# Second products of twelve chunks with the output weights held still, in a fused attention and feed-forward kernel

## The chip, the cores and the metric

The kernel runs on one core of one Trainium2 chip. The metric is the device time of one execution in microseconds (us). Before the change it is 499.11 us, the median of three runs (498.87 to 499.72).

## What is computed

First a gated linear attention is run over 768 steps, for 4 batches of 8 heads of size 48. Its output, 3072 tokens of 384 numbers, goes through a feed-forward layer with 2048 hidden units.

```python
for t in range(S):                                   # attention, per batch and head
    state = alpha[:, :, t, :, None] * state + einsum('bhd,bhe->bhde', k[:, :, t], v[:, :, t])
    y[:, :, t] = einsum('bhd,bhde->bhe', q[:, :, t], state)
x = y.transpose(0, 2, 1, 3).reshape(3072, 384)
h = x @ w_in                                         # 384 -> 2048
sp = where(h > 20, h, log1p(exp(min(h, 20))))
out = (h * tanh(sp)) @ w_out                         # 2048 -> 384
```

## The kernel before

**Chunks and units.** The tokens are cut into 24 chunks of 128 columns (64 steps of two batches). A chunk goes through `attention` (VectorE scans of the decay, small matmuls, a state that is carried on), which leaves its 128 columns of `x` in SBUF as a high and a low part (fp32r). The feed-forward layer works in *units*: one block `f` of 128 hidden features (16 of them, `NFF`) for a group of 2 or 4 chunks. There are 100 units. `SEGMENTS` (line 42) lists which groups go over which blocks: chunks 0 to 7 in six pieces (units 0 to 35), since weights and chunks come in one after the other, then chunks 8 to 11, 12 to 15, 16 to 19 and 20 to 23 with all 16 blocks each (units 36 to 51, 52 to 67, 68 to 83, 84 to 99).

**One unit** (`unit`, line 1004). The *first product* (`up`, line 1013) is 9 matmuls: three pieces of the 384 inputs, each as high x high, high x low and low x high. The weights stand still and 512 columns (256 for a group of two) stream. Five ScalarE and VectorE passes make the gate (lines 1026 to 1046), then ScalarE writes the high part of `g` (line 1051) and VectorE the low part (line 1054). The *second product* (`down`, line 1085) is done chunk by chunk: the chunk's 128x128 piece of `g` stands still and the 384 columns of the output weights `wo` stream, three passes per chunk, so 12 matmuls in a unit of four chunks. The sums stay in four PSUM banks (`o0` to `o3`, one for each chunk) over a segment. After the last block ScalarE copies a bank to SBUF with a check sum (`result`, line 1125) and SyncE stores it (line 1131); chunks 0 to 7, whose blocks are spread over segments, are put aside in between (`stash`, `more`, `join`).

**Weights.** They come as 64-bit words (768 KB for a block). VectorE puts the top bits together (lines 428, 433 and 438), ScalarE rounds the high part (line 449), and the low part is the rest. `W_LOW` (line 82) says for each block who computes the low part: `PE` subtracts by two matmuls into a PSUM bank, done once for the input weights and once for the output weights (lines 467 and 468), `POOL` by two GpSimd instructions (line 477), `DVE` by one VectorE instruction (line 455). All weights are loaded once more for a check in the background (line 485).

**Variants of a chunk.** Chunks in `DIRECT` write `x` in place by more matmuls with separate pieces (lines 742 and 781); the others send 16-row pieces through small DMAs (`move`, line 855). In `X_PE` TensorE and ScalarE make the low part of `x` (`off`, line 840) and not VectorE. In `STATE_PE` TensorE adds the state (line 807).

**Order.** `Plan.order` (line 149) goes through all tasks with durations (`COST`) and due times (`key`, with the shifts `DUE_SHIFT`, `W_SHIFT`, `LEAD` and others) and writes down one fixed order for each engine; where its count leaves TensorE idle in the first part it puts in *fills*, matmuls without use (line 1160). The engines then run their orders and wait for each other by semaphores. A unit's second product is due `LAG` = 3 units after its first.

Of the kernel before, what the change touches and what calls it, by code (L numbers as in the profile page):

```python
# [30 lines left out]
P = 128  # L31
# [22 lines left out]
LEAD = 5.5  # L54
SPREAD = 3.0
W_LEAD = 4.25
GATE = -2.0
Q_LEAD = 4.75
V_LEAD = 9.75
FIRST_W = -22.25  # L60
CHECK_FROM = 105
# [5 lines left out]
DUE_SHIFT = {  # L67
# [3 lines left out]
}  # L71
W_SHIFT = {
    0: -30.0, 1: -2.75, 2: -3.75, 3: -1.75, 4: -3.5, 5: -9.25, 6: 0.25, 7: -4.75, 8: 2.5, 9: 2.75,
    10: 2.25, 11: 7.0, 12: -6.25, 13: -7.75, 14: 30.25, 15: -1.75,
}
X_PE = {0, 1}
SIDES = 2
STATE_PE = {2, 6}
PAIR_FROM = 8
BACK_AFTER = 0.8  # L80
# [6 lines left out]
MOVER = {  # L87
    (1, 1, 0): 'ACT', (1, 2, 0): 'ACT', (1, 2, 64): 'ACT', (2, 1, 0): 'ACT', (2, 2, 64): 'ACT',
    (3, 0, 64): 'ACT', (3, 1, 64): 'ACT', (3, 2, 64): 'ACT', (4, 0, 0): 'ACT', (5, 1, 0): 'ACT',
    (6, 0, 0): 'ACT', (6, 0, 64): 'ACT', (6, 2, 64): 'ACT', (8, 0, 0): 'ACT', (8, 1, 64): 'ACT',  # L90
}
# [30 lines left out]
class Plan:  # L122
# [151 lines left out]

KEYS = 60.0
PER_KEY = {'PE': 0.03, 'DVE': 0.02, 'ACT': 0.02, 'POOL': 0.02, 'SP': 0}

# [10 lines left out]
    "front": (1.19, 1.32), "front d": (1.59, 1.72), "front0": (0.76, 0.9), "turn": (0.34, 0.6), "turn2": (0.7, 0.95),  # L288
    "front2": (2.09, 2.22), "back2": (1.91, 2.04), "back2 last": (1.18, 1.3), "spread": (0.4, 0.4),
# [3 lines left out]
    "down": (0.529, 0.8), "stash": (0.4, 0.53), "join": (0.47, 0.59), "result": (0.5, 0.7),  # L293
}
# [15 lines left out]
def fast_path(ctx, tc, qka, v, w, out, good):  # L310
# [48 lines left out]
    gchk = const.tile([P, NFF], F32, name="gchk")  # L359
    n_last = n_chunks - SEGMENTS[-1][1]  # L360
    ws = const.tile([P, 2, NFF, 2, DM], F32R, name="ws")
    wi = ws[:, :, :, 0].rearrange("p z f (s c) -> p z f s c", s=NK)
# [235 lines left out]
    def chunk(n):  # L598
# [54 lines left out]
        if n == 0:  # L653
            got_a, got_k, got_q = (
                add("SP", *COST["load"], -99 + 0.1 * i, load_part(*e), uses=[q_buf], size=230)
                for i, e in enumerate(((a_at, QKA), (k_at, a_at), (0, k_at)))
            )
        elif n < PARTED:
            got_a, got_k = (
                add("SP", *COST["load"], key - Q_LEAD - early, load_part(*e), uses=[q_buf], size=z)  # L660
                for z, e, early in ((230, (a_at, QKA), 1.0), (460, (0, a_at), 0.0))
            )
            got_q = got_k
        else:
            got_a = got_k = got_q = add(
                "SP", *COST["load"], key - Q_LEAD, load, uses=[q_buf], size=692
            )
# [149 lines left out]
        x = xs[tile_at]  # L817
        by_half = lambda t: t.rearrange("p s (t u) -> p u s t", u=2)
        sides = (
# [182 lines left out]
    by_token = out.rearrange("(b t) d -> t b d", t=S)  # L1002

    def unit(c0, nt, f, at, ends):
        N, key = nt * C, float(at)
# [69 lines left out]
        t_lo = add("DVE", *cost("dve"), k + 0.07, lower, [t_hi], [y, g], port=at >= IN_BANK)  # L1075

        for j in range(nt):
            n = c0 + j
# [24 lines left out]
            if f < NFF - 1 and n in kept:  # L1103
                def more(o=o, n=n):
                    nc.vector.tensor_tensor(part[n].tile, o.tile, part[n].tile, ALU.add)

                kept[n] = add("DVE", *COST["join"], k, more, [t_down, kept[n]], [o, part[n]])
                continue
            if f < NFF - 1:
                part[n] = plan.buffer("osb")  # L1110

                def stash(o=o, n=n):
                    nc.scalar.copy(new(part[n], [P, DM], f"part{n}"), o.tile)

# [3 lines left out]
            if from_part:  # L1118
                def join(o=o, n=n):
                    nc.vector.tensor_tensor(part[n].tile, o.tile, part[n].tile, ALU.add)  # L1120

                done = [add("DVE", *COST["join"], k, join, [t_down, kept[n]], [o, part[n]])]
            osb = part[n] if from_part else plan.buffer("osb")

            def result(o=o, n=n, osb=osb, from_part=from_part):
                to = osb.tile if from_part else new(osb, [P, DM], f"osb{n}")
                nc.scalar.activation(
# [3 lines left out]
            def store(n=n, osb=osb):  # L1131
                b, c = chunks[n]
                nc.sync.dma_start(by_token[c * L : (c + 1) * L, 2 * b : 2 * b + 2], osb.tile)

# [8 lines left out]
            def copy(on_act=on_act, o=o, n=n, osb=osb):  # L1143
                to = new(osb, [P, DM], f"osb{n}")
                if on_act:
# [4 lines left out]
            def send(n=n, osb=osb):  # L1150
                b, c = chunks[n]
                queue = nc.scalar if n == n_chunks - 1 else nc.sync
                queue.dma_start(by_token[c * L : (c + 1) * L, 2 * b : 2 * b + 2], osb.tile)

# [245 lines left out]
def lay_out(inputs):  # L1400
# [62 lines left out]
```

## Time and profile before

| | us |
|---|---|
| median of three runs | 499.11 |
| the profiled execution, its own time | 497.71 |
| its span in the profile | 496.0 |
| TensorE busy | 484.6 (98%) |
| ScalarE busy | 382.1 (77%) |
| VectorE busy | 323.1 (65%) |
| GpSimd busy | 25.3 (5%) |

The span runs from the first to the last instruction of the core; 1.71 us of the profiled execution's time lie around it. Busy time of TensorE is that of matmuls whose ends are modelled, and they overlap; how long one really takes of the engine is read from the starts of those that follow each other. "Granted clock" is the share of 2.4 GHz that TensorE got; over the span its mean is 0.998.

### The profile page before, as it was taken

To read this page: it belongs to the slowest core of one execution; us is meant where nothing else is said; L and a number is where in the kernel's file an instruction comes from. 1 tells how busy PE (TensorE), PEld (TensorE's weight loads), DVE (VectorE), ACT (ScalarE), POOL (GpSimd) and SP (SyncE) were. 2 spreads that over 40 slices of the span, in tenths; PEclk is the share of its full clock that TensorE was granted. 3 is DMA by queue.
4 is the path that set the end of the run, shared out by engine and by line. 5 is a ranking of instruction groups with operands and counts; after the bars stand their busy time and mean duration, and the time that the engine had idled before them with its cause. 6 is when DMAs were issued, how large, how long until landed. Compare 5 with 4: busy or idle time off the path is not lost.

```text
span 496.0 us, 12822 instructions
## 1 busy us (share of the span) xinstructions
PE 484.6 (98%) x5319; PEld 432.5 (87%) x5319; DVE 323.1 (65%) x522; ACT 382.1 (77%) x864; POOL 25.3 (5%) x27
## 2 busy tenths in 40 slices
PE   6999999999999999999999999999999999999995
PEld 4688889899899989999989899999989899999994
DVE  7999999999973694447867783863474343343333
ACT  3578786886788778857777897889789899997772
POOL 2003201413000000000000000000000000000000
PEclk9999999999999999999999999999999999999999
DMA  7877544606000250115152543603153412100001
GB/s 248 316 285 236 181 151 157 238 35 214 13 0 9 78 172 1 66 59 175 28 213 75 183 164 99 207 24 118 71 171 93 172 41 106 64 1 0 1 0 68
DMA packets 18926, 56.22 MB, mean 113 GB/s; under 512 B 3440, under 2 KB 11312, under 8 KB 18864
## 3 DMA queue, kind: packets, MB, share of 16 engines
q1 hardware_dynamic: 18592, 55.11, 32.5%
q8 instruction: 42, 0.69, 0.6%
q10 hardware_dynamic: 272, 0.26, 0.2%
q14 instruction: 20, 0.16, 0.1%
HBM read 48.87 MB, written 4.72 MB: 108 GB/s over the span
## 4 chain that ended last, share of the span: by engine, by line
PE 85%; DVE 9%; DMA 3%; issue 1%; ACT 1%; SPq 0%; DVEq 0%; ACTq 0%
PE sums_at L1089 39%; PE h_at L1017 37%; PE att_at L790 2%; PE att_at L752 2%; DVE w_lead L433 2%; PE h_at L763 2%; DMA ws<-in_wp_dram 1%; DVE w_lead L438 1%; PE att_at L724 1%; DMA qka<-in_qka_dram 1%; PE h_at L802 1%; DVE w_lead L428 1%; DVE t L1044 1%; DVE g L1054 1%; DVE rest L672 1%
## 5 line engine op out<-in xcount | busy, mean ns | idle before, releaser
L1089 PE MATMUL sums_at<-ws,g 128*128 128x384 f32 x1152 | 223.9, 340 | 0.1
L1017 PE MATMUL h_at<-xs,ws 128*128 128x512 f32 (+1 forms) x900 | 214.2, 384 | 0.2 <-DVE t L1044 0.2
L1089 PEld LDWEIGHTS sums_at<-ws,g 128*128 128x128 f32 x1152 | 202.4, 188 | 8.1 <-ACT ws L471 0.4
L1017 PEld LDWEIGHTS h_at<-xs,ws 128*128 128x128 f32 x900 | 163.3, 188 | 28.4 <-DVE t L1044 0.5
L1054 DVE SCALAR_TENSOR_TENSOR g<-t,g 128x512 fp32r<-128x512 f32 (+1 forms) x100 | 67.8, 679 | 124.2 <-ACT g L1051 123.9
L1026 ACT ACTIVATE t<-h_at 128x512 f32<-128x512 f32 (+1 forms) x100 | 58.0, 580 | 63.6 <-PE h_at L1017 60.8
L1051 ACT ACTIVATE g<-t 128x512 fp32r<-128x512 f32 (+1 forms) x100 | 60.3, 604 | 11.5 <-PE sums_at L1089 5.3
L1029 ACT ACTIVATE t<-t 128x512 f32<-128x512 f32 (+1 forms) x100 | 61.3, 613 | 2.3
L1032 ACT ACTIVATE t<-t 128x512 f32<-128x512 f32 (+1 forms) x100 | 61.2, 612 | 2.2
L1044 DVE SCALAR_TENSOR_TENSOR t<-t,h_at 128x512 f32<-128x512 f32 (+1 forms) x87 | 57.1, 657 | 8.3 <-ACT t L1035 8.2
L1035 ACT ACTIVATE t<-t 128x512 f32<-128x512 f32 (+1 forms) x100 | 60.4, 604 | 0.5
L672 DVE TENSOR_TENSOR_SCAN rest<-qka,behind 112x520 f32<-112x520 f32 x24 | 30.4, 1268 | 0.4 <-DMA qka<-in_qka_dram 0.2
L685 DVE TENSOR_TENSOR_SCAN qka<-qka,ahead 112x520 f32<-112x520 f32 x24 | 30.6, 1274 | 0.0
L477 POOL TENSOR_TENSOR ws<-w_lead,ws 128x384 fp32r<-128x384 f32 x14 | 22.1, 1598 | 98.3 <-ACT ws L449 98.3
L1026 ACT ACTIVATION_READ_ACCUMULATOR t<-h_at 128x1 f32 x100 | 19.4, 194 | 0.0
L1041 DVE COPY held<-h_at 128x512 f32<-128x512 f32 x13 | 9.0, 691 | 15.8 <-ACT t L1026 15.8
L831 ACT ACTIVATE xs<-att_at 112x384 fp32r<-112x384 f32 (+1 forms) x24 | 12.2, 513 | 6.2 <-PE att_at L809 3.4
L695 DVE TENSOR_TENSOR qka<-qka 112x512 f32<-112x512 f32 x24 | 16.4, 684 | 0.1
L681 DVE TENSOR_TENSOR qka<-qka,rest 112x512 f32<-112x512 f32 x24 | 15.8, 659 | 0.0
L433 DVE SCALAR_TENSOR_TENSOR w_lead<-ws,w_lead 128x768 int32<-128x768 int32 x16 | 15.7, 982 | 0.1
L438 DVE SCALAR_TENSOR_TENSOR w_lead<-ws,w_lead 128x768 int32<-128x768 int32 x16 | 15.3, 957 | 0.1
L449 ACT ACTIVATE ws<-w_lead 128x768 fp32r<-128x768 f32 x16 | 13.4, 839 | 2.3 <-DVE w_lead L438 2.2
(100 smaller groups left out, 366.7 us busy)
## 6 DMA issues: line engine op xcount, KB each, us to landing
qka<-in_qka_dram SPq DMA_DIRECT2D x22, 772.5 KB, 5.8
ws<-in_wp_dram SPq DMA_DIRECT2D x16, 768.0 KB, 4.5
wc<-in_wp_dram SPq DMA_DIRECT2D x16, 768.0 KB, 4.5
v<-in_vp_dram SPq DMA_DIRECT2D x24, 192.0 KB, 4.5
out_dram<-osb SPq DMA_DIRECT2D x15, 192.0 KB, 2.6
xs<-x SPq DMA_DIRECT2D x104, 16.0 KB, 1.8
out_dram<-part SPq DMA_DIRECT2D x8, 192.0 KB, 2.6
qka<-in_qka_dram SPq DMA_DIRECT2D x2, 260.5 KB, 4.4
```

The costliest lines, as they stand in the source:

```text
L433: nc.vector.scalar_tensor_tensor(lead.tile, words(1), -0x40000000, lead.tile, ALU.bitwise_and, ALU.bitwise_or)
L672: nc.vector.tensor_tensor_scan(t[:, :0:-1], alpha()[:, :0:-1], behind[:, ::-1], 0.0, ALU.mult, ALU.max)
L685: nc.vector.tensor_tensor_scan(a, a, ahead, 0.0, ALU.mult, ALU.max)
L1017: nc.tensor.matmul(p[:, :N].rearrange("p (c t) -> p c t", c=nt), wi[:, z, f, s], x[:, :, s, a], start=m == 0, stop=m == len(passes) - 1,)
L1026: nc.scalar.activation(wide(t), wide(h), AF.Exp, accum_out=vchk[:, at : at + 1])
L1029: nc.scalar.activation(wide(t), wide(t), AF.Square, bias=1.0)
L1032: nc.scalar.activation(wide(t), wide(t), AF.Ln, bias=0.2, scale=0.2)
L1035: nc.scalar.activation(wide(t), wide(t), AF.Exp, scale=-1.0)
L1044: nc.vector.scalar_tensor_tensor(wide(y), wide(t), 2.5, wide(held), ALU.subtract, ALU.mult)
L1051: nc.scalar.activation(g.tile[:, 0, :N], wide(y), AF.Copy, scale=-0.4, accum_out=own)
L1054: nc.vector.scalar_tensor_tensor(g.tile[:, 1, :N], wide(y), -0.4, g.tile[:, 0, :N].bitcast(F32), ALU.mult, ALU.subtract,)
L1089: nc.tensor.matmul(o.tile, g.tile[:, a, j * C : (j + 1) * C], wo[:, z, f], start=begins and m == 0, stop=end and m == 2,)
```

## The change

For chunks 8 to 19 (`WIDE`, the groups that begin at 8, 12 and 16) the second product is turned round: 128 output columns of `wo` stand still, the 512 tokens of the group stream, and the result has outputs in its partitions and tokens in its columns. Three banks of 512 columns are used and not four of 384. After the last block VectorE transposes each bank in squares of 32 (`flip`) into a tile of the group, ScalarE makes the check sums over two chunks at a time, and 16 stores of 48 KB take the place of four of 192 KB. So that a square of 32 lands where it can be stored, the host lays the output weights out in another order of columns; the second products that are not turned then read `wo` in 12 runs of 32 columns, and for the three groups the columns of `x` are ordered half by half. SBUF tiles for results hold four chunks (two such tiles in place of eight single ones).

The planner's numbers and choices are set anew as well: due times, costs of loads, and who does what for the early chunks and weights.

```diff
 BUFS = {
-    "h": 2, "t": 3, "g": 2, "osb": 8,
+    "h": 2, "t": 3, "g": 2, "osb": 2,
...
-X_PE = {0, 1}
+X_PE = {0, 1, 2, 4}
-STATE_PE = {2, 6}
+STATE_PE = {2, 3, 4, 6}
-DIRECT = {0, 1, 2, 3, 6, 7}
+DIRECT = {1, 2, 3, 6}
 W_LOW = {
-    0: ('PE', 'o0'), 1: ('PE', 'o0'), 2: ('PE', 'o3'), 3: ('PE', 'o3'), 4: ('POOL', ''), 5: ('PE', 'o0'),
-    6: ('DVE', ''), 7: ('POOL', ''), 8: ('POOL', ''), 9: ('DVE', ''), 10: ('DVE', ''), 11: ('POOL', ''),
-    12: ('POOL', ''), 13: ('POOL', ''), 14: ('DVE', ''), 15: ('POOL', ''),
+    0: ('PE', 'h'), 1: ('PE', 'o3'), 2: ('PE', 'o0'), 3: ('POOL', ''), 4: ('POOL', ''), 5: ('PE', 'o3'),
+    6: ('POOL', ''), 7: ('POOL', ''), 8: ('DVE', ''), 9: ('POOL', ''), 10: ('POOL', ''),
+    11: ('POOL', ''), 12: ('DVE', ''), 13: ('POOL', ''), 14: ('POOL', ''), 15: ('DVE', ''),
 }
+WIDE = {8, 12, 16}
-FLIGHT = 1800.0
+FLIGHT = 3000.0
-DMA_RATE, DMA_FIRST, DMA_LAST = 285.0, 1.1, 0.9
+DMA_RATE, DMA_FIRST, DMA_LAST = 345.0, 1.7, 0.6
...
+        within = "u t" if n // NT_MOST * NT_MOST in WIDE else "t u"
+        by_half = lambda t: t.rearrange(f"p s ({within}) -> p u s t", u=2)
...
+    def wide_products(c0, f, key, g, t_lo):
+        begins, end = f == 0, f == NFF - 1
+        if begins:
+            sums[c0] = [plan.buffer(f"o{i}") for i in range(NK)]
+        turned = out_buffer(c0) if end else None
+        blocks = lambda: out_rows(c0, 4).rearrange("p k (q i e) -> p (k q) i e", i=NK, e=32)
+        flips = []
+        for i, o in enumerate(sums[c0]):
+            def down(o=o, i=i):
+                if begins:
+                    o.tile = sums_at[i]
+                for m, (a, z) in enumerate(((0, 0), (0, 1), (1, 0))):
+                    nc.tensor.matmul(
+                        o.tile, wo[:, z, f, i * P : (i + 1) * P], g.tile[:, a],
+                        start=begins and m == 0, stop=end and m == 2,
+                    )
+            def flip(o=o, i=i):
+                nc.vector.transpose(blocks()[:, :, i], o.tile.rearrange("p (b t) -> p b t", t=32))
...
+        for c in range(2):
+            def check(c=c):
+                rows = out_rows(c0 + 2 * c, 2)
+                nc.scalar.activation(rows, rows, AF.Copy, accum_out=ochk[:, c0 + c : c0 + c + 1])
...
+            for a in range(4):
+                for h in range(2):
+                    def store(a=a, c=c, h=h):
+                        of = blocks()[32 * a : 32 * (a + 1), 8 * c + h : 8 * (c + 1) : 2]
+                        nc.sync.dma_start(
+                            by_block[:, a, c0 // 2 + c, :, h], of.rearrange("p b i e -> p b (i e)")
+                        )
...
+        if c0 in WIDE:
+            wide_products(c0, f, key, g, t_lo)
+            return
...
                     nc.tensor.matmul(
-                        o.tile, g.tile[:, a, j * C : (j + 1) * C], wo[:, z, f],
+                        o.tile.rearrange("p (r i e) -> p r i e", r=4, i=NK),
+                        g.tile[:, a, j * C : (j + 1) * C],
+                        wo[:, z, f].rearrange("p (i r e) -> p r i e", r=4, i=NK),
...
-    wp[:, :, 1] = w_out.reshape(NFF, P, DM)
+    wp[:, :, 1] = (
+        w_out.reshape(NFF, P, 4, NK, 32).transpose(0, 1, 3, 2, 4).reshape(NFF, P, DM)
+    )
```

Three places show what this moves.

TensorE in the group of chunks 12 to 15, second products of units 55 and 56 (`g55`, `g56` are the units' gates, `sums_at` the PSUM banks, `h_at` the bank of a first product). Before:

```order
L1089 MATMUL sums_at0_106<-ws_103,g55_3759 128x384 x3
L1017 MATMUL h_at0_111<-xs1_105,ws_103 128x512 x9
L1089 MATMUL sums_at1_107<-ws_103,g55_3759 128x384 x3
L1089 MATMUL sums_at2_108<-ws_103,g55_3759 128x384 x3
L1089 MATMUL sums_at3_109<-ws_103,g55_3759 128x384 x3
L1089 MATMUL sums_at0_106<-ws_103,g56_3804 128x384 x3
L1017 MATMUL h_at1_112<-xs1_105,ws_103 128x512 x9
```

With the change:

```order
L1036 MATMUL sums_at0_107<-g55_3692,ws_104 128x512 x3
L1086 MATMUL h_at0_112<-xs1_106,ws_104 128x512 x9
L1036 MATMUL sums_at1_108<-g55_3692,ws_104 128x512 x3
L1036 MATMUL sums_at2_109<-g55_3692,ws_104 128x512 x3
L1036 MATMUL sums_at0_107<-g56_3737,ws_104 128x512 x3
L1086 MATMUL h_at1_113<-xs1_106,ws_104 128x512 x9
```

A unit of these groups has three second products of 512 columns and not four of 384. Over the whole program 576 matmuls of 384 columns become 432 of 512, and 576 stay.

GpSimd, low parts of weights (`w_lead4` is block 4). Before:

```order
L477 TENSOR_TENSOR ws_103<-w_lead4_659,ws_103 128x384 x2
L477 TENSOR_TENSOR ws_103<-w_lead7_698,ws_103 128x384 x2
L477 TENSOR_TENSOR ws_103<-w_lead8_1083,ws_103 128x384 x2
L477 TENSOR_TENSOR ws_103<-w_lead13_1339,ws_103 128x384 x2
L477 TENSOR_TENSOR ws_103<-w_lead12_1438,ws_103 128x384 x2
L477 TENSOR_TENSOR ws_103<-w_lead15_1600,ws_103 128x384 x2
L477 TENSOR_TENSOR ws_103<-w_lead11_1623,ws_103 128x384 x2
```

With the change:

```order
L479 TENSOR_TENSOR ws_104<-w_lead3_516,ws_104 128x384 x2
L479 TENSOR_TENSOR ws_104<-w_lead4_608,ws_104 128x384 x2
L479 TENSOR_TENSOR ws_104<-w_lead6_702,ws_104 128x384 x2
L479 TENSOR_TENSOR ws_104<-w_lead7_868,ws_104 128x384 x2
L479 TENSOR_TENSOR ws_104<-w_lead9_1178,ws_104 128x384 x2
L479 TENSOR_TENSOR ws_104<-w_lead10_1251,ws_104 128x384 x2
L479 TENSOR_TENSOR ws_104<-w_lead11_1362,ws_104 128x384 x2
L479 TENSOR_TENSOR ws_104<-w_lead13_1526,ws_104 128x384 x2
L479 TENSOR_TENSOR ws_104<-w_lead14_1773,ws_104 128x384 x2
```

Blocks 3, 6, 9 and 10 come to GpSimd, from TensorE and VectorE; block 8 goes to VectorE. Before, five blocks stood here ahead of the last two, now seven.

VectorE where the group of chunks 8 to 11 ends, with the change (`osb2` is the tile of that group's results, `STREAM_TRANSPOSE` the flip, `t` and `g` the gates of units 52 and 53; `copy_predicated` serves the attention of chunks 18 and 19):

```order
L1110 COPY held53_3415<-h_at1_113 128x512
L1042 STREAM_TRANSPOSE osb2_3488<-sums_at0_107 128x16x32
L1123 SCALAR_TENSOR_TENSOR g52_3421<-t52_3391,g52_3421 128x512
L1113 SCALAR_TENSOR_TENSOR t53_3409<-t53_3409,held53_3415 128x512
L585 COPY_PREDICATED probs_90<-causal_79,h_at0_112 128x2x256
L585 COPY_PREDICATED probs_90<-causal_79,h_at1_113 128x2x256
L1042 STREAM_TRANSPOSE osb2_3488<-sums_at1_108 128x16x32
L1042 STREAM_TRANSPOSE osb2_3488<-sums_at2_109 128x16x32
```

The three flips stand among the gates of the next group's first units; before, nothing of the results of these chunks was on VectorE.

Counted over the program, TensorE also has two subtractions of weights fewer (8 pairs of lines 467 and 468 in place of 10), two additions of a state more, eight small matmuls of line 844 more (12 in place of 4), and 32 fills in place of 31.

## Rows read from the trace of the kernel before

**Rows 1.** The page: busy time of each engine over the span.
```profile
PE 484.6 (98%) x5319; PEld 432.5 (87%) x5319; DVE 323.1 (65%) x522; ACT 382.1 (77%) x864; POOL 25.3 (5%) x27
```
**Rows 2.** Stretches: length, then busy (instructions) of PE, PEld, DVE, ACT, POOL, clock, DMA.
```profile
45.00:95.00 50.00, 49.99 (x793) 44.34 (x793) 49.15 (x77) 39.10 (x94) 13.82 (x8) 1.00 0.55 195
...
400.00:489.00 89.00, 89.00 (x454) 81.22 (x452) 30.95 (x60) 72.46 (x165) 0.00 (x0) 1.00 0.09 30
```
**Rows 3.** The waits of PE, the longest and the last of five: us, times, longest.
```profile
PE sums_at L1165 <- ACT minus_ident L336: 2.8, 1, 2.8
...
PE h_at L1017 <- DVE t L1044: 0.2, 1, 0.2
```
**Rows 4.** The chain that ended last, from 400 us: start, us, what.
```profile
400.76 2.05 PE h_at L1017 x9
402.81 2.10 PE sums_at L1089 x12
404.91 2.08 PE h_at L1017 x9
406.99 2.12 PE sums_at L1089 x12
```
**Rows 5.** PE in order of time from 26 us: start, us, what.
```profile
26.09 0.91 PE L467 MATMUL sums_at<-w_lead,ident 128*128 128x384 f32 x2
...
27.01 0.81 PE L467 MATMUL sums_at<-w_lead,ident 128*128 128x384 f32 x2
...
27.83 0.84 PE L467 MATMUL sums_at<-w_lead,ident 128*128 128x384 f32 x2
...
29.97 0.91 PE L809 MATMUL att_at<-state,ident 112*112 112x192 f32 x4
30.58 0.66 PE L1017 MATMUL h_at<-xs,ws 128*128 128x256 f32 x3
```
**Rows 6.** PE again: line 844, then `back` of a direct chunk, then of another.
```profile
14.35 0.51 PE L844 MATMUL att_at<-xs,minus_ident 128*128 128x192 f32 x2
14.68 0.57 PE L724 MATMUL sums_at<-ident,qka 112*128 112x112 f32 x4
...
28.77 0.58 PE L783 MATMUL att_at<-probs,v_apart 64*64 64x64 f32 x24
...
29.50 0.54 PE L802 MATMUL att_at<-v,ks 64*48 64x48 f32 x32
...
49.14 0.69 PE L790 MATMUL att_at<-probs,v 64*64 64x64 f32 x32
49.63 0.56 PE L802 MATMUL att_at<-v,ks 64*48 64x48 f32 x32
```
**Rows 7.** Groups of PE by line and shape: the fills (busy us, mean ns, idle before).
```profile
L1165 PE MATMUL sums_at<-minus_ident 128*128 128x512 f32 x31 | 10.5, 466 | 2.8 <-ACT minus_ident L336 2.8
```
**Rows 8.** DVE from 71.57 us, and POOL beside it: start, us, what.
```profile
71.57 1.23 DVE L672 TENSOR_TENSOR_SCAN rest<-qka,behind 112x520 f32<-112x520 f32 x1
...
75.67 2.06 DVE L685 TENSOR_TENSOR_SCAN qka<-qka,ahead 112x520 f32<-112x520 f32 x1
...
73.91 2.71 POOL L477 TENSOR_TENSOR ws<-w_lead,ws 128x384 fp32r<-128x384 f32 x2 [21.48 <-ACT ws L449]
```
**Rows 9.** Groups of DVE and ACT by line and shape (busy us, mean ns, idle before).
```profile
L1041 DVE COPY held<-h_at 128x512 f32<-128x512 f32 x13 | 9.0, 691 | 15.8 <-ACT t L1026 15.8
...
L455 DVE TENSOR_TENSOR ws<-w_lead,ws 128x768 fp32r<-128x768 f32 x4 | 3.8, 954 | 0.0
...
L874 DVE TENSOR_TENSOR state<-att_at,state 112x384 f32<-112x384 f32 x4 | 2.2, 552 | 0.0
...
L837 DVE TENSOR_TENSOR xs<-att_at,xs 128x384 fp32r<-128x384 f32 x4 | 2.2, 549 | 0.0
...
L500 ACT ACTIVATE wc<-wc 128x768 f32<-128x768 f32 x16 | 14.6, 915 | 0.0
```
**Rows 10.** Stores of line 1133 on SyncE's queue: min/median/max ns, first and last start.
```profile
L1133 SPq DMA_DIRECT2D out_dram<-osb x12: 539/601/909, 276.1 to 432.2; - x12
```

More of the change, by code (lines that the diff above doesn't have):

```diff
@@ L292 @@
     "x3 hi": (0.16, 0.3), "x3 lo": (0.2, 0.32), "x hi": (0.39, 0.53), "x lo": (0.48, 0.59),
-    "down": (0.529, 0.8), "stash": (0.4, 0.53), "join": (0.47, 0.59), "result": (0.5, 0.7),
+    "down": (0.529, 0.8), "down wide": (0.687, 0.95), "flip": (0.66, 0.8), "sum": (0.87, 1.0), "stash": (0.4, 0.53), "join": (0.47, 0.59), "result": (0.5, 0.7),
 }
@@ L660, in chunk @@
                 add("SP", *COST["load"], key - Q_LEAD - early, load_part(*e), uses=[q_buf], size=z)
-                for z, e, early in ((230, (a_at, QKA), 1.0), (460, (0, a_at), 0.0))
+                for z, e, early in ((267, (a_at, QKA), 1.0), (524, (0, a_at), 0.0))
             )
@@ L1002, in fast_path, with out_buffer, out_rows @@
     by_token = out.rearrange("(b t) d -> t b d", t=S)
+    out_buffers = {}
+    def out_buffer(n):
+        group = n // NT_MOST
+        if group not in out_buffers:
+            out_buffers[group] = plan.buffer("osb")
+        return out_buffers[group]
+    def out_rows(n, count=None):
+        of, place = out_buffer(n), n % NT_MOST
+        if of.tile is None:
+            new(of, [P, NT_MOST, DM], f"osb{n // NT_MOST}")
+        return of.tile[:, place : place + count] if count else of.tile[:, place]
@@ new lines, in fast_path @@
+    by_block = out.rearrange("(b c h t) (a e) -> t a c b h e", b=B, c=NCH, h=2, a=4)
+    def wide_products(c0, f, key, g, t_lo):
[16 more added lines that the diff above has]
+                nc.vector.transpose(blocks()[:, :, i], o.tile.rearrange("p (b t) -> p b t", t=32))
+            t_down = add(
+                "PE", *COST["down wide"], key + LAG + 0.001 * i, down, [t_lo, *ready_w[f, 1]],
+                [g, o], behind=downs.get((c0, i), []), steps=6,
+            )
+            downs[c0, i] = [t_down]
+            if end:
+                flips.append(
+                    add("DVE", *COST["flip"], key + LAG + 0.1 + 0.01 * i, flip, [t_down], [o, turned])
+                )
+        if not end:
+            return
[3 more added lines that the diff above has]
+                nc.scalar.activation(rows, rows, AF.Copy, accum_out=ochk[:, c0 + c : c0 + c + 1])
+            t = add("ACT", *COST["sum"], key + LAG + 0.2 + 0.1 * c, check, flips, [turned])
+            checked.append(t)
+            for a in range(4):
[4 more added lines that the diff above has]
+                            by_block[:, a, c0 // 2 + c, :, h], of.rearrange("p b i e -> p b (i e)")
+                        )
+                    add("SP", *COST["store"], key + LAG + 0.3 + 0.1 * c, store, [t], [turned])
@@ L1104, in more @@
                 def more(o=o, n=n):
-                    nc.vector.tensor_tensor(part[n].tile, o.tile, part[n].tile, ALU.add)
+                    nc.vector.tensor_tensor(out_rows(n), o.tile, out_rows(n), ALU.add)
                 kept[n] = add("DVE", *COST["join"], k, more, [t_down, kept[n]], [o, part[n]])
@@ L1109, in unit @@
             if f < NFF - 1:
-                part[n] = plan.buffer("osb")
+                part[n] = out_buffer(n)
                 def stash(o=o, n=n):
-                    nc.scalar.copy(new(part[n], [P, DM], f"part{n}"), o.tile)
+                    nc.scalar.copy(out_rows(n), o.tile)
                 kept[n] = add("ACT", *COST["stash"], k, stash, [t_down], [o, part[n]])
@@ L1119, in join @@
                 def join(o=o, n=n):
-                    nc.vector.tensor_tensor(part[n].tile, o.tile, part[n].tile, ALU.add)
+                    nc.vector.tensor_tensor(out_rows(n), o.tile, out_rows(n), ALU.add)
                 done = [add("DVE", *COST["join"], k, join, [t_down, kept[n]], [o, part[n]])]
-            osb = part[n] if from_part else plan.buffer("osb")
+            osb = out_buffer(n)
             def result(o=o, n=n, osb=osb, from_part=from_part):
-                to = osb.tile if from_part else new(osb, [P, DM], f"osb{n}")
+                to = out_rows(n)
                 nc.scalar.activation(
@@ L1143, in copy @@
             def copy(on_act=on_act, o=o, n=n, osb=osb):
-                to = new(osb, [P, DM], f"osb{n}")
+                to = out_rows(n)
                 if on_act:
```

40 lines of the change are left out of this document (21 added, 19 removed), and 6 rows, old and new, of the table DUE_SHIFT.

## The prediction

> **What bounds the kernel now.** I read the busy line of the page first: TensorE is busy for 484.6 of the span's 496.0 us, no other engine for more than 382.1 [rows 1]. Then the stretches, because a share over the span says nothing of a stage: from 45 to 95 us TensorE and VectorE are both full (49.99 and 49.15 of 50), from 400 to 489 TensorE is full, VectorE is at 30.95 of 89 and ScalarE at 72.46 [rows 2]. Then TensorE's waits: five lines that add up to 5.5 us, the longest 2.8 on the first constant, all early [rows 3]. Last the chain of waits, where the reader is to see that it is TensorE alone, a first product of 2.05 to 2.08 us and a second one of 2.10 to 2.12 in turn, each starting where the other ends [rows 4]. So the time is the length of TensorE's work, plus 11.4 us (496.0 - 484.6) in which it has none, plus 1.7 outside the span. Work taken from TensorE counts in full as long as nobody makes it wait. In the first 100 us VectorE has only 0.85 us in 50 to spare; there an edit is worth what it takes from both.
>
> **The change part by part.** The sum is made against the profiled execution, 497.71 us; the median of the three runs is 1.40 higher, and I add that at the end.
>
> *(a) Turned products.* A unit of chunks 8 to 19 now has 9 matmuls of 512 columns and not 12 of 384. The nearest row is the first product of the same kernel: also 128x128 held, 512 streaming, 9 in a run. It takes 2.065 us (mean of 2.05 and 2.08), the 12 take 2.11 [rows 4]: 229 and 176 ns for one. Both stream 4608 columns, so the difference is what a matmul costs beside its columns, about 16 ns, paid three times less. 0.045 us in each of 48 units: **-2.16 us**. The bounds are 0 (only the columns count) and -2.9 (2.12 against 2.06). I take the middle, since the form is that of the first product exactly.
>
> The Trainium skill, "TensorE: Matmul & The Clock Gate", section "Wait — 56ns, not 53.3ns?", speaks against this: it has matmuls start every N/2.4 GHz plus about 2.5 ns, so that 9 of 512 would take an estimated 1.94 us and 12 of 384 1.95, and the 48 units would give 0.4 us. The trace disagrees with it in both rows (2.065 and 2.11); the measurement decides, and the rule is a rival below.
>
> *(b to f) TensorE's other work, in the first 100 us.* Two pairs of weight subtractions go: the starts 26.09, 27.01 and 27.83 make one 0.82 to 0.92 [rows 5], so 2 x 0.87 = -1.74. Two chunks more (3 and 4) add their state on TensorE: 29.97 to 30.58 is 0.61 each [rows 5], +1.22. Line 844, 0.33 for a pair of matmuls [rows 6], comes for chunks 2 and 4; a chunk that is not direct (4, and now 0) has a second part a third as wide, 0.11: 2 x 0.33 + 2 x 0.11 = +0.88. Chunks 0 and 7 are no longer direct: a direct `back` takes 0.73 (28.77 to 29.50), another 0.49 [rows 6]; chunk 0 changes once and chunk 7 twice, counting its front, for which I take the same 0.24: -0.72. One fill more: 10.5/31 = +0.34 [rows 7]. Together -0.02: nothing.
>
> *VectorE in the first stretch.* Two state additions (0.55 each), two low parts of `x` (0.55) and two low parts of weights (0.95) fewer [rows 9]: -4.1 us. Against that GpSimd has seven early blocks and not five. Beside GpSimd a scan took 2.06 us and not 1.23 [rows 8], and one block lies on GpSimd for 2.71; with one scan beside each, 2 x 0.83 = +1.7, with two +3.3. Net -2.4 to -0.8: room for VectorE, but by the order it comes late. Ahead of the gates of units 7 to 12 VectorE now has two to six instructions more than before, and fewer only from unit 16 on. I cost this at nothing for TensorE: the lead of a few instructions is given back by unit 16, and TensorE has work of other chunks between those gates. Where that cover is gone, it is the first rival.
>
> *Flips.* Nine new instructions on VectorE. None is in the trace; the nearest are the copy of 512 columns out of PSUM, 691 ns [rows 9], and the scan of 520, 1.23 us [rows 8]. Below: nothing less than the copy, since as many numbers leave the same memory. I take 0.69, 6.2 us in all, and hold 1.23 for the range (11.1 us). What is queued behind them are the gates of the next group's first units, and behind those TensorE's second products, which have three units of slack. The cover is that stage's idle time of VectorE (35% busy without attention [rows 2]; 65% over the span [rows 1]), and that TensorE comes back to a bank only after a first product (2.07) or attention work. If the cover is gone, TensorE waits at the three group ends for one flip each: 3 x 0.69 to 1.23 = 2.1 to 3.7.
>
> *Checks and stores.* Two ScalarE passes over twice the columns take the place of four results per group: as much work, nothing. 48 stores of 48 KB replace 12 of 192 KB. Issuing one took 0.54 to 0.91 us, median 0.60, on SyncE's queue [rows 10]; 16 hold it for about 9.6 us per group where four held it 2.4. What stands behind them there are loads of weights to be checked and of later chunks' inputs, which TensorE needs many units later: nothing. Ten more small `x` moves, six of them issued by ScalarE, at the same 0.6 would be 3.6 us there while ScalarE is at 39.10 of 50 [rows 2]: hidden. Weight checks are due later than before: nine passes of 0.92 [rows 9] now fall into units 84 to 96, where ScalarE is idle for 16.5 us in 21 units, 0.78 in each; nine units with one each fall behind by 9 x 0.14 = 1.2 us. The three units of lag cover that; without cover it is +1.2.
>
> *Strided `wo`.* The 576 products left as they were read the output weights in 12 runs of 32 columns. The nearest row on one side is the first product, which reads `x` in four runs of 128 at the same price per column: 0. On the other side line 844 reads every second column: 0.165 us for 192 columns, where the price of (a) gives 80 + 16 ns [rows 6]; at that rate, +0.07 per 192 columns, 576 matmuls of 384 would cost +80 us. I take 0, because runs of 32 are far nearer to runs of 128 than to runs of one.
>
> **Sum.** -2.16 - 0.02 = -2.18: 497.71 becomes 495.5, and with the 1.40 between that execution and the median, **496.9 us**.
>
> **The rivals.**
>
> *R1, the first stretch becomes longer: slower.* VectorE is full there and the scans pay for GpSimd. Mechanism: gates of units 7 to 12 come late, TensorE waits, and since it has no idle time afterwards nothing is made up. Price: 1.7 for the scans and two to six instructions of 0.64 us (49.15/77 [rows 2]), mean 2.6: +4.3, hence 501.2. It decides from 3.2 us on (2.2 of the gain and 1.0 beyond). For it: VectorE at 98%. Against it: VectorE's total falls by up to 2.4 us, and only five short waits of TensorE stand in the trace of before. 0.13.
>
> *R2, strided `wo` is not free.* From 3.8 ns per matmul on (2.2 us/576) the gain is gone, from 5.6 on the kernel is measurably slower; at 10 ns it is 496.9 + 5.8 = 502.7. For it: line 844. Against it: the first product's runs. 0.04.
>
> *R3, the gain is eaten at the three group ends.* TensorE meets a bank that is not yet flipped: +2.1 to +3.7, that is 499.0 to 500.6, most likely near 499.0, since a copy from PSUM takes 0.69. For it: three banks, not four, and flips that stand behind gates in the order. Against it: the order puts first products and attention between them. 0.13.
>
> *R4, the first stretch becomes shorter as well.* VectorE's -0.8 to -2.4 there come out where both engines pace the work, or part of the 11.4 us without work goes, since loads and due times are set anew: a further -1.4 to -3.4, that is 493.5 to 495.5. Against it: TensorE's own work there does not shrink, and its waits are 5.5 in all, 2.8 of them on the first constant. 0.16.
>
> *R5, only columns count.* Should a turned product take 2.11 like the old one, because the 16 ns hang on something other than the number of matmuls, (a) is 0 and the time 499.1. The two rows [rows 4] stand against it. 0.04. The Trainium skill's rule in the section named above would give an estimated 498.7 in this case.
>
> **How the numbers follow.** The forecast has 0.50, R1 0.13, R2 0.04, R3 0.13, R4 0.16, R5 0.04. About 0.2%, 1.0 us, is what a measurement can tell from no change. Faster by more than that are the forecast and R4, 0.66; within it R3 and R5, 0.17; slower R1 and R2, 0.17. The range goes from R4's end with the scatter of the runs (493.0) to above R3's far end (500.8), and leaves out R1 and R2.
>
> **What would show it right or wrong.** The chain from 400 us is as before, since chunks 20 to 23 are not turned: 2.06 and 2.11 (if the 12 take longer, R2). Between 200 and 400 us a turned product of 9 takes 2.06 to 2.07 (2.11: R5). TensorE's busy time falls by about 2.2. Its waits stay near 5.5 us, with none on a flip (R3) and none in the first 100 us that is longer than now (R1). A flip takes 0.69 to 1.23 us. Unit 36's first product, the first one after chunks 0 to 7, begins when it did before; 1.4 us or more earlier is R4, and 3 us or more later R1. A time outside 495.9 to 497.9 with all of these right would mean that I have left out a term.

## The result and the profile after

The change makes the kernel slower: 501.64 us (median of 9 runs, 500.48 to 503.0) against 498.54 (9 runs, 497.39 to 499.72), ratio 1.0066, interval 1.005 to 1.0082. The forecast was 496.9, the range 493.0 to 500.8. The profiled execution of the change took 502.75 us, 1.1 above its median; that of before lay 0.8 below its own. So 1.9 of the 5.0 us between the two profiles are scatter, and only what comes back in several executions is used below.

The busy line of the page, for [rows 1]:

```profile
PE 486.6 (97%) x5138; PEld 415.0 (83%) x5138; DVE 326.0 (65%) x522; ACT 387.7 (77%) x855; POOL 34.4 (7%) x32
```

Stretches, for [rows 2]: in the first one VectorE has become a little emptier (48.24 for 49.15) and GpSimd fuller.

```profile
45.00:95.00 50.00, 49.94 (x762) 44.18 (x761) 48.24 (x76) 39.30 (x94) 18.28 (x10) 1.00 0.54 179
400.00:489.00 89.00, 89.00 (x426) 77.87 (x425) 31.70 (x55) 82.64 (x181) 0.00 (x0) 1.00 0.22 72
```

TensorE's waits, for [rows 3]: two are new and long, and one of them has no releaser ("issue").

```profile
PE sums_at L1240 <- ACT minus_ident L337: 2.9, 1, 2.9
PE sums_at L1036 <- DVE state L702: 1.7, 1, 1.7
PE h_at L1086 <- issue: 1.0, 1, 1.0
PE att_at L792 <- DVE probs L780: 0.8, 1, 0.8
```

The chain, for [rows 4], first in a turned group, then in the last one, which is not turned:

```profile
401.55 2.08 PE h_at L1086 x9
403.63 2.06 PE sums_at L1036 x9
...
434.57 2.06 PE h_at L1086 x9
436.63 2.12 PE sums_at L1162 x12
```

A turned product takes 2.06 as forecast, but the first product beside it takes 2.08 or 2.09.

**Where the time went.** I cut the span at the first products of units 36 and 98 (the groups of chunks 8 to 23, without the end). Row of before, then of the change; columns as in [rows 2]:

```profile
188.66:475.72 287.06, 287.06 (x2816) 259.99 (x2816) 150.53 (x249) 235.29 (x526) 0.00 (x0) 1.00 0.28 92
```

```profile
190.78:480.38 289.60, 286.73 (x2671) 239.63 (x2671) 154.66 (x254) 238.02 (x513) 0.00 (x0) 1.00 0.28 91
```

Here the change should have gained, and it loses 2.54 us; TensorE is idle for 2.87 us of the stretch, before for none. Summing the time from each matmul's start to the next: second products 133.32 before, 131.54 after; first products 127.98 and 130.05; attention 25.76 and 28.01. Two idle pieces, at 283.24 and 317.66 us, make up 2.72 of the 2.87; a third, of 0.15, is at 257.46.

### The profile page after: what moved, and what is told of

Read it like the earlier page. It is cut to its first block, busy times and chain, and to the rows that moved or that the text cites. A ratio compares the mean times of both kernels' runs of the same rounds, so it can differ in the third digit from the quotient of the medians.

```text
span 501.0 us, 12517 instructions
## 1 busy us (share of the span) xinstructions
PE 486.6 (97%) x5138; PEld 415.0 (83%) x5138; DVE 326.0 (65%) x522; ACT 387.7 (77%) x855; POOL 34.4 (7%) x32
## 4 chain that ended last, share of the span: by engine, by line
PE 88%; DVE 4%; DMA 3%; ACT 1%; issue 1%; SPq 1%; DVEq 0%
PE h_at L1086 39%; PE sums_at L1036 20%; PE sums_at L1162 20%; DMA ws<-in_wp_dram 3%; PE att_at L792 2%; PE att_at L754 2%; PE h_at L765 1%; PE att_at L726 1%; PE h_at L804 1%; DVE w_lead L435 1%; DVE w_lead L430 1%; DVE w_lead L440 1%; DVE rest L674 0%; DVE probs L780 0%; DVE state L702 0%
## 5 line engine op out<-in xcount | busy, mean ns | idle before, releaser
L1123 DVE SCALAR_TENSOR_TENSOR g<-t,g 128x512 fp32r<-128x512 f32 (+1 forms) x100 | 66.4, 665 | 110.5 <-ACT g L1120 110.5
L1162 PE MATMUL sums_at<-ws,g 128*128 128x384 f32 x576 | 112.6, 343 | 0.0
L1036 PE MATMUL sums_at<-g,ws 128*128 128x512 f32 x432 | 110.2, 396 | 1.7 <-DVE state L702 1.7
L1162 PEld LDWEIGHTS sums_at<-ws,g 128*128 128x128 f32 x576 | 101.7, 188 | 3.7
L1036 PEld LDWEIGHTS sums_at<-g,ws 128*128 128x128 f32 x432 | 79.9, 188 | 19.4 <-DVE state L702 1.9
L1113 DVE SCALAR_TENSOR_TENSOR t<-t,h_at 128x512 f32<-128x512 f32 (+1 forms) x91 | 60.0, 660 | 25.3 <-ACT t L1104 23.0
L479 POOL TENSOR_TENSOR ws<-w_lead,ws 128x384 fp32r<-128x384 f32 x18 | 31.1, 1746 | 100.4 <-ACT ws L451 100.4
L792 PEld LDWEIGHTS att_at<-probs,v 64*48 64x48 f32 (+1 forms) x736 | 12.9, 126 | 4.8 <-issue 1.7
L792 PE MATMUL att_at<-probs,v 64*48 64x64 f32 (+1 forms) x736 | 15.6, 220 | 0.9 <-DVE probs L780 0.8
```

What stands on the lines that cost most here:

```text
L479: nc.gpsimd.tensor_tensor(lo[:, m], both()[:, m], hi[:, m].bitcast(F32), ALU.subtract)
L792: nc.tensor.matmul(y[64 * a : 64 * a + wide, u, j], V()[own, h : h + wide], probs[slot][own, a, j], start=first and j == 0 and not direct ...
L1036: nc.tensor.matmul(o.tile, wo[:, z, f, i * P : (i + 1) * P], g.tile[:, a], start=begins and m == 0, stop=end and m == 2,)
L1113: nc.vector.scalar_tensor_tensor(wide(y), wide(t), 2.5, wide(held), ALU.subtract, ALU.mult)
L1123: nc.vector.scalar_tensor_tensor(g.tile[:, 1, :N], wide(y), -0.4, g.tile[:, 0, :N].bitcast(F32), ALU.mult, ALU.subtract,)
L1162: nc.tensor.matmul(o.tile.rearrange("p (r i e) -> p r i e", r=4, i=NK), g.tile[:, a, j * C : (j + 1) * C], wo[:, z, f].rearrange("p (i r e ...
```

## The experiments

Theories at first: *N*, the new numbers lengthen the first stretch and turning gains; *T*, turning itself costs.

**1. Turned alone.** All numbers and choices as before, `WIDE` kept (likewise W_LOW, MOVER, DUE_SHIFT, W_SHIFT, the leads, DMA rates and loads' sizes):

```diff
-X_PE = {0, 1, 2, 4}
+X_PE = {0, 1}
-STATE_PE = {2, 3, 4, 6}
+STATE_PE = {2, 6}
-FLIGHT = 3000.0
+FLIGHT = 1800.0
-PER_KEY = {'PE': 0, 'DVE': 0.02, 'ACT': 0.02, 'POOL': 0.2, 'SP': 0.2}
+PER_KEY = {'PE': 0.03, 'DVE': 0.02, 'ACT': 0.02, 'POOL': 0.02, 'SP': 0}
...
```

> The turned products of chunks 8 to 19 with all numbers and choices of the planner as they were before. Theory N (the new numbers and choices lengthen the first stretch, turning itself gains): TensorE's order up to unit 36 is that of before, so unit 36 starts at 192.9 us within 0.5, each pair of products in the turned groups takes 4.15 us and not 4.18, and the time is 1 to 2 us below before (ratio 0.996 to 0.998). Rival T (turning itself costs, by flips that stand ahead of TensorE's work and by instruction loading): 1 to 3 us above before, ratio 1.002 to 1.006, with waits of TensorE at the ends of the groups.

Measured: 506.48 us (503.0 to 511.31), ratio 1.0171 (1.0126 to 1.0216). Neither theory has the size. The profiled execution is the quickest of the six (503.0).

**2. Not turned.** New numbers, no group turned.

```diff
-WIDE = {8, 12, 16}
+WIDE = set()
```

> The change with no group turned (12 products of 384 columns everywhere), all new numbers and choices kept. Theory N: unit 36 still starts about 2 us later than before (195 us), and the time is 3 to 5 us above before (ratio 1.006 to 1.010), no better than the change as a whole. Rival T: the loss is gone, the time is within 1 us of before.

Measured: 503.56 us, ratio 1.0092 (1.0059 to 1.0125). Unit 36 starts at 189.85, but from there to unit 98 it takes 290.46 us, 3.4 more than before; 1.76 of that is idle time, 1.11 at 241.73 and 0.61 at 266.35 the longest. The time is about what N said, the place is not.

**3. The code alone.** Both edits: old numbers, not turned.

> No group turned and all numbers and choices as before: left of the change are the order of the columns of the output weights (12 runs of 32 columns are read), the tiles for results and the stores' place. TensorE's and VectorE's orders are those of before. Theory N and rival T both: within 0.5 us of before (12 products of 384 columns take 2.117 us in place of 2.109 in the changed kernel's last group, 0.008 x 96 = 0.8 us at most). Rival S (the strided reading or the result tiles cost): 1 to 3 us above before.

Measured: 498.99 us, ratio 1.0005 (0.9986 to 1.0024). From unit 36 to 98:

```profile
190.37:477.88 287.51, 287.51 (x2815) 260.66 (x2815) 150.61 (x249) 235.14 (x525) 0.00 (x0) 1.00 0.28 92
```

0.45 us more than before: second products 133.93 for 133.32. The strided output weights cost about 0.6 us over 744 products, 0.8 ns each.

**4. The change again.**

> The change as it is, beside the three others on the same chip. Theory N and rival T both: ratio 1.005 to 1.008, as measured; unit 36 starts 2 us later than before. If N and T both hold in part, the differences of the other three to this one add up to it.

Measured: 502.31 us, ratio 1.0076 (1.005 to 1.0101). The wait before line 1036 is there again, at 284.96 us (1.71 us), and the one inside a first product at 319.36 (0.70); a third, 1.00, is at 258.34. (The first profile has 0.15 at that third place.) The waits come back in a second execution, though not with the same length.

What held up experiment 1 is read from its trace. SyncE's queue near 365 us, then VectorE:

```profile
361.51 8.42 SPq L1067 DMA_DIRECT2D out_dram<-osb  x16
370.03 0.38 SPq L643 DMA_DIRECT2D qka<-in_qka_dram  x1
```

```profile
374.84 1.24 DVE L674 TENSOR_TENSOR_SCAN rest<-qka,behind 112x520 f32<-112x520 f32 x1 [1.65 <-DMA qka<-in_qka_dram]
```

The 16 stores stand ahead of a load of `qka`; the scan of that chunk waits for it; the gates behind the scan come late, and TensorE waits 1.13 us at 377.5. After unit 36 three such scans wait for a load, 1.28, 2.18 and 1.65 us, and TensorE is idle for 2.33 us. In the change the same load was issued at 357.6, ahead of the stores: the new numbers had moved it. That gave theories *Q* (SyncE's queue) and *F* (flips).

**5. Loads first.** Experiment 1 with the stores due later, and SyncE's choices after unit 36 weighted by due time. TensorE's order stays the same.

```diff
+                    late = 3.0 + 0.4 * (8 * c + 2 * a + h)
-                    add("SP", *COST["store"], key + LAG + 0.3 + 0.1 * c, store, [t], [turned])
+                    add("SP", *COST["store"], key + LAG + late, store, [t], [turned])
...
+                    per_key = 0.3 if e == 'SP' and low > 36 else PER_KEY[e]
```

> The turned products with the planner's numbers of before, as in the first experiment, TensorE's order unchanged; only the 16 stores of a group now stand behind the loads and moves of the next chunks on SyncE's queue. Theory Q (the stores of 48 KB held up the loads of qka on SyncE's queue, VectorE's scans came late, TensorE waited): the waits of VectorE on qka after unit 36 are gone, TensorE has no wait over 0.3 us after 100 us, and the time falls from 506 to 497 to 498.5 (ratio to before 0.997 to 1.000). Rival F (flips among the gates delay TensorE): stays above 502.

Measured: 498.81 us, ratio 0.9985 (0.9963 to 1.0007): 7.7 us below experiment 1. SyncE's queue in the same place:

```profile
358.92 0.93 SPq L1068 DMA_DIRECT2D out_dram<-osb  x2
359.96 0.36 SPq L644 DMA_DIRECT2D qka<-in_qka_dram  x1
360.37 3.32 SPq L1068 DMA_DIRECT2D out_dram<-osb  x7
366.37 1.22 SPq L653 DMA_DIRECT2D v<-in_vp_dram  x2
```

The stretch from unit 36 to 98:

```profile
190.39:476.62 286.23, 286.23 (x2671) 239.46 (x2671) 157.51 (x258) 237.53 (x513) 0.00 (x0) 1.00 0.29 92
```

No idle time, and no scan waits for a load of `qka`. It is 1.28 us less than experiment 3, which has the same numbers and is not turned. Second products give 2.23 (133.93 to 131.70), first products take 0.87 back (127.82 to 128.69). A wait of 0.68 us at 96.5 us, which the expectation excluded only after 100 us, stands in before too with 0.23.

**6. Four stores.** Experiment 1 with 4 stores of 192 KB per group.

```diff
-            for a in range(4):
-                for h in range(2):
...
+            for n in (c0 + 2 * c, c0 + 2 * c + 1):
+                def store(n=n):
+                    nc.sync.dma_start(by_token[n // 2 * L : (n // 2 + 1) * L, 2 * (n % 2) : 2 * (n % 2) + 2], out_rows(n))
```

> The first experiment's kernel with 4 stores of 192 KB per group in place of 16 of 48 KB; the stores write the turned blocks as they lie, so the output's places differ from the reference's. TensorE's order is unchanged. Theory Q (SyncE's queue): SyncE is held for 2.4 us per group and not 8.4, and the time falls from 506 to 497 to 499. Rival F (flips): stays above 502.

Measured: 499.29 us, ratio 1.0018 (0.9992 to 1.0045); 286.48 from unit 36 to 98. Two scans still wait for a load, 1.00 and 0.83 us, and TensorE does not. F falls: the nine flips stand at the same places of VectorE's order, between the same neighbours, in 1, 5 and 6. Q holds, with two limits. In 5 and 6 the planner also sets other instructions of VectorE and ScalarE in another order (in both a scan of `rest` stands a few places earlier), so more than the stores differs. And between the profiled executions of 1 and 5 lie 3.9 us (503.0 and 499.13); the rest of the 7.7 is in executions of experiment 1 without a trace.

**7. Fills in two.** Now the change's own waits. The profile names VectorE's line 702 as the releaser of the long one. But in the program that second product of unit 52 waits for a flip, which ended at 281.14, and a matmul amid a first product waits for nothing. TensorE in order of time:

```profile
282.65 0.57 PE L804 MATMUL h_at<-v,ks 64*48 64x48 f32 x31
284.96 0.97 PE L1036 MATMUL sums_at<-g,ws 128*128 128x512 f32 x3 [1.74 <-DVE state L702]
```

```profile
315.63 2.02 PE L1086 MATMUL h_at<-xs,ws 128*128 128x512 f32 x8
318.63 2.47 PE L1086 MATMUL h_at<-xs,ws 128*128 128x512 f32 x10 [0.98 <-issue]
```

The DMA view of the 0.1 us from 282.6 shows what began just ahead (queue, packets, MB, share):

```profile
q8 instruction: 1, 0.02, 59.2%
```

On this queue come blocks of 16,384 bytes. One began at 282.64, one at 316.42; TensorE went on 2.32 and 2.21 us later, and in experiment 4 2.38 to 2.68 us after such a block began. Hence theory *I*: TensorE waits for its own instructions, and where depends on where a block ends. To move the ends without moving an order, each matmul without use became two:

```diff
-                spare.tile.rearrange("p (j t) -> p j t", j=NPAIR), minus_ident,
+            for j in range(0, NPAIR, NPAIR // 2):
...
```

> The change, with each of the 32 matmuls without use in the first 45 us split in two of 256 columns: the same orders, but every later instruction of TensorE lies 64 places further on. Theory I (the waits of 0.7 to 1.9 us at 258, 284 and 318 us, 2.2 to 2.7 us after a block of TensorE's instructions began to load, are waits for instructions and depend on where a block ends): these waits vanish or come at other places of the program, the sum of them changes by over 1 us and the time with it. Rival D (they are waits for data of VectorE, as the inferred releaser of one of them says): the same waits at the same places, 2.5 to 3.5 us in all.

Measured: 499.75 us, ratio 1.0012 (0.9988 to 1.0037), 2.6 below experiment 4 and 1.9 below the first measurement of the change. From unit 36 to 98, then the place of the long wait:

```profile
193.34:480.51 287.17, 286.74 (x2671) 239.65 (x2671) 154.44 (x254) 237.87 (x513) 0.00 (x0) 1.00 0.29 92
```

```profile
285.19 0.57 PE L804 MATMUL h_at<-v,ks 64*48 64x48 f32 x32
285.69 0.97 PE L1036 MATMUL sums_at<-g,ws 128*128 128x512 f32 x3
```

The wait before line 1036 is gone, 0.43 us of idle time is left of 2.87 (0.14 and 0.29, both among attention's small matmuls), and the stretch is 2.43 us shorter. Theory I holds; D falls. (The late start, 193.34, is one wait of 1.6 us for a move of `x` in this execution, which took 503.09, and the lower clock behind it, granted clock 0.50 from 28 to 30 us.)

**8. Fills in four.**

> As the one before, with each of these matmuls in four of 128 columns: later instructions lie 192 places further on. Theory I: the waits at 258, 284 and 318 us vanish or are at other places than both in the change and in the kernel with two parts. Rival D: the same waits at the same places.

Measured: 509.95 us, ratio 1.0208 (1.016 to 1.0256). Unit 36 starts at 200.64, since matmuls of 128 columns cost more than the columns say:

```profile
22.90 4.16 PE L1241 MATMUL sums_at<-minus_ident 128*128 128x128 f32 x36
```

111 ns for 128 columns (26.90 less 22.90, by 36), where one of 512 takes about 230. The expectation had no price for that. From unit 36 to 98 it is 287.46 us, with 0.78 idle at 268.5 and 369.3: the waits went elsewhere, as I said.

**9. Loads first, fills in two.**

> The kernel of the fifth experiment (no wait for instructions in its profile), with the matmuls without use split in two of 256 columns: same orders, TensorE's later instructions 64 places further on. Theory I (waits for instructions come from where the blocks end, not from turning): waits of TensorE without a late releaser, 2.1 to 2.7 us after a block began to load, may now appear between 200 and 400 us, and the time rises by as much, 0 to 3 us above 498.8. Rival D (such waits belong to the change's numbers): none appear, 498.8 within 0.6.

Measured: 498.54 us, ratio 1.0004 (0.999 to 1.0018); again 286.23 from unit 36 to 98, no idle time. It does not tell I from D: this shift too leaves the ends harmless.

**10. Half of the fills in two** (the first 16).

> The change with 16 of the 32 matmuls without use split in two: 32 places further on. Theory I: the sum of the waits for instructions after unit 36 differs from the change's (2.9 and 3.4 us) and from that with all 32 split (0.4 us), since the blocks end 32 places earlier in the attention's rows of small matmuls; anything from 0 to 4 us, and the time is 499 to 503, moving with that sum. Rival D: waits at 258, 284 and 318 us as in the change.

Measured: 503.58 us (4 runs, 502.21 to 504.73), ratio 1.0108 (1.0081 to 1.0135). The profiled execution, the quickest of the four, idles 1.98 us in the stretch, between 0.43 and 2.87, at 282.9 and 314.3; none at 258. The stretch follows (288.71), the median does not: it is above the change's, and the three executions above 502.21 have no trace.

**11. Not turned, fills in two.**

> The second experiment's kernel (new numbers, no group turned; 503.6 us) with all matmuls without use split in two. Theory I: its waits at 241 (1.1 us) and 266 (0.6 us) go or move; from unit 36 to unit 98 it takes 283 to 284.5 us and not 286.3, and the time is 500.5 to 502, 1 to 1.5 above the seventh experiment (499.75), which is what turning is then worth. Rival N (the new numbers themselves cost 3 us or more): stays at 503 or above.

Measured: 504.13 us, ratio 1.0111 (1.009 to 1.0133): no gain, against the expectation. The wait of 0.61 us at 266 has not moved (it is at 269.7, before the same first product: a wait for a gate). The other has moved to 239 us and grown:

```profile
240.87 0.40 PE L804 MATMUL h_at<-v,ks 64*48 64x48 f32 x16 [1.87 <-issue]
```

and TensorE's clock falls behind it:

```profile
242.00:244.00 2.00, 2.00 (x7) 1.72 (x7) 1.97 (x6) 0.00 (x0) 0.00 (x0) 0.50 0.38 105
244.00:246.00 2.00, 2.00 (x8) 1.58 (x7) 1.97 (x4) 0.00 (x0) 0.00 (x0) 0.66 0.07 18
```

That is the lower of its two levels, 1.2 GHz: six matmuls of 512 columns take 0.43 us each and not 0.23, two of 384 columns 0.32 and not 0.18, so this adds some 1.5 us. What the new numbers cost without such waits is not separated by this run.

**What 2, 4, 8, 10 and 11 show together.** Counting TensorE's matmuls up to a wait tells I from D. From the start to a moment within each of the two long waits, TensorE's busy time and matmuls, clock and DMA, first in the change, then in experiment 10, where 16 more matmuls stand ahead:

```profile
0.00:283.90 283.90, 277.45 (x3525) 1.00 0.37 126
0.00:318.20 318.20, 310.14 (x3908) 1.00 0.38 129
```

```profile
0.00:283.50 283.50, 276.43 (x3525) 1.00 0.37 126
0.00:314.90 314.90, 306.66 (x3908) 1.00 0.38 129
```

The number is the same, and the place of the program is 16 matmuls earlier: in the change the wait at 3525 stands before a second product, in experiment 10 among attention's small matmuls.

```profile
284.10 0.40 PE L804 MATMUL h_at<-v,ks 64*48 64x48 f32 x16 [1.16 <-issue]
315.15 0.29 PE L804 MATMUL h_at<-v,ks 64*48 64x48 f32 x5 [0.82 <-issue]
```

It is 2890 in both experiments 2 and 11, though 32 more matmuls stand ahead in 11; 3145, 3525 and 3908 in experiment 4; 3525 and 3908 in what is left of idle time in 7; 4416 in 8. These numbers lie 255, 380, 383 and 508 apart, which is 2, 3, 3 and 4 times some 127, and 41 blocks come for the change's 5138 matmuls. A wait for data would stay at its place of the program; these stay at block ends. What decides when a block begins to load was not tried.

**12. Before again.**

> The kernel before, once more with a profile, to see how much the start of unit 36 differs between executions of it. If the first stretch of the new code is longer than that of before, unit 36 starts at 188.7 us again within 0.5; if the profile of before was an early execution, it starts at 189.5 to 191, as in all kernels of this study (190.2 to 191.0 with the old numbers, 189.9 to 191.7 with the new ones). From unit 36 to unit 98 it takes 287.1 us within 0.2 in both cases.

Measured: 498.76 us; unit 36 starts at 189.67 and not at 188.66, and it takes 287.06 from there to unit 98, as in the first profile. So the first profile of before was an early execution.

## Why the prediction was wrong

**What bounds the kernel: right.** TensorE fills both stages, and every idle piece after unit 36 is in the time.

**(a), the turned products: the size of their own term was right, the sum was not.** Predicted -2.16; experiments 3 and 5 differ by -2.23 in second products. What the term left out is the first product beside a turned one: 2.063 us there without turning, 2.085 with it (medians in experiments 3 and 5), +0.87 in all; in the change's last group, which is not turned, it is 2.06 again (at 434.57 us above). Turning is worth 1.3 us, 0.03 in a unit and not 0.045. **R5** did not happen: a turned product takes 2.06 us and not 2.11, and a matmul of 512 or 384 columns costs about 16 ns beside its columns. By the rule of the Trainium skill, "TensorE: Matmul & The Clock Gate", section "Wait — 56ns, not 53.3ns?", the 48 units would give an estimated 0.4 us. The 2.23 measured in second products speaks against it.

**(b to f): the work came out even as summed.** Unit 36 starts at 190.2 to 191.0 in experiments 1, 3, 5, 6 and 9, with the old numbers, and at 189.9 to 191.7 in the change's two executions and experiments 2, 10 and 11, with the new ones. So neither **R1**, my rival for "slower" (3 us or more later), nor **R4** (1.4 us or more earlier) happened: VectorE has 48.24 of 50 in the critical stretch, and TensorE 49.94. The price that R1 put on the scans fell on other instructions: in the first 195 us the scans take 1.27 us in the mean (1.29 before), but twelve state additions take 750 ns and not 548, first before, then with the change (busy us, mean ns, idle before):

```profile
L700 DVE TENSOR_TENSOR state<-state,rest 112x384 f32<-112x384 f32 x12 | 6.6, 548 | 0.0
```

```profile
L702 DVE TENSOR_TENSOR state<-state,rest 112x384 f32<-112x384 f32 x12 | 9.0, 750 | 0.0
```

Why all kernels with the new code start unit 36 later than before's two executions (188.66, 189.67), most by 1 to 2 us, stays open; over the whole program the code alone is worth 0.5 us, within its interval.

**The step that failed: the sum held only TensorE's work and its waits for data.** TensorE also waits for its own instructions: 2.87 us of idle time in the change's profile and 3.41 in its second, none before. The sum put this at nothing, without a word on it. Nothing in my reading of the trace of before covers it, since before has no such wait; but its DMA table lists the queue they come on, and I passed over it (packets, MB, share):

```profile
q8 instruction: 42, 0.69, 0.6%
```

The source that I had names them too. `Plan.order` counts TensorE's instructions in blocks of 256 (line 98 of the kernel before) and adds a delay where a block comes late (lines 244 to 249). Whether its count fits the program was not tested.

A turned unit has three matmuls and three weight loads fewer (2671 matmuls from unit 36 to 98 for 2816), and the new choices shift everything before it, so that blocks end elsewhere among the attention's rows of 128 small matmuls. Each long wait stands in such a row or at most 16 matmuls behind it. Experiment 7 removes most of the waits with the same orders, and 1.9 to 2.6 us of the time; the block numbers of experiments 2, 10 and 11 show that the waits belong to block ends. Turning is not their cause by itself: experiment 2, which is not turned, has one of 1.11 us, and experiments 1, 5, 6 and 9, which are turned with the old numbers, have none.

The Trainium skill, "Runtime: NRT & Kernel Launch", section "Instruction fetch mechanics", says that instructions come in blocks of 16 KiB on a DMA queue of the sequencer's own and that crossing a block's end is mostly hidden. The traces agree on the blocks (16,384 bytes); in the change the end was not hidden.

**Stores: "nothing" was wrong as a rule and right in this change.** With the old numbers the time falls by 7.7 us when they stand behind the loads (experiments 1 and 5). The traces show one way, a load behind them on SyncE's queue that VectorE needed at once, not "many units later"; what of the 7.7 goes this way is shown for the profiled executions alone, which lie 3.9 apart. In the change the new due times issue that load first.

**Flips: right.** None of TensorE's matmuls waited for one.

```profile
L1042 DVE STREAM_TRANSPOSE osb<-sums_at x9: 674/709/718, 277.2 to 434.1; 128x512 f32<-128x512 f32 x9
```

0.71 us, near the lower bound of 0.69; **R3** did not happen.

**Strided `wo`, R2: right to leave out**, 0.8 ns for each product against a break-even of 3.8. But the far end of its range was misread: line 844's 0.165 us for 192 columns is not all the price of a stride, because short matmuls are dear in themselves: 128 columns in a row take 111 ns (experiment 8) and 256 take 127 (experiment 7).

**The account.** Taken from start to start, the waits are longer than the idle time, because part of each lies under the modelled end of the matmul ahead. The matmuls ahead of the three waits take 0.35, 1.95 and 1.37 us to the next start, where others like them take 0.01 to 0.02 us among the small ones and 0.23 in a first product: some 3.4 us in all. So from unit 36 to 98 the change has -1.78 in second products, +0.9 in first ones beside turned ones, and +3.4 in waits for instructions: the measured +2.54. Without the waits the stretch would take an estimated 286.2 us (289.60 - 3.4), 0.8 less than before and the same as in experiments 5 and 9 (286.23). With the later start of unit 36 the 2.54 gives the measured 3.1 within the scatter.

Experiment 7, where 0.8 of the 3.4 is left, equals before within its interval, and the turned products with the old numbers and loads first do too (0.9985, 0.9963 to 1.0007): a version that is clearly quicker than both was not found.

## What to carry to other kernels

An edit that alters how many instructions an engine runs moves the ends of its instruction blocks; if the engine has rows of very short instructions, look at every wait without a plausible releaser, and whether an instruction block began to load some 2 us before it ended (2.2 to 2.7 us here). Count the instructions up to the wait: if an edit further ahead leaves the count and moves the place, the wait is not for data. When one large transfer becomes many small ones on a queue, list what is queued behind them and when that is needed, also where it is for an engine that is not the bound. Cut the span at the same piece of work in both kernels before comparing: it separates scatter at the start from what the change does.

## What was not expected of the hardware

- A wait's named releaser can be chance: line 702 ended 0.08 us before TensorE went on, and had nothing to do with it.
- Matmuls of the same form differ by neighbour: the first product of 9 x 512 columns takes 2.060 to 2.063 us beside 12 x 384 and 2.085 to 2.086 beside 9 x 512 (medians of every profile). Why was not tried.
- Matmuls in a row, at the higher clock: 128 columns take 111 ns, 256 take 127 (18 in 2.29 us in experiment 7), 512 take about 230.
- A wait of 1.87 us was followed by the lower level of the clock (0.50 from 242 to 244 us) in experiment 11, and one of 1.61 us in experiment 7 (0.50 from 28 to 30 us); one of 1.74 us in the change was not (granted clock 1.00 behind it). What decides it is not shown.
